# Means sent for a step sooner, a query pair turned by VectorE, wo rounded behind the gated tiles

## The chip, the cores and the metric

The kernel runs on one core of a Trainium2 chip. A core has five engines with a queue each: TensorE (PE, with its weight loads shown apart as PEld), VectorE (DVE), ScalarE (ACT), GpSimd (POOL) and SyncE (SP, which issues DMAs only). The metric is the device time of one execution in microseconds (us), lower is better.

## The reference

Two blocks read the same layer-normed input, and both are added to it. S = 2048 rows, D = 512, 32 heads of 16, the gated block 1376 wide.

```python
xn = _layernorm(x)
q, k, v = split(xn @ wqkv)                        # 32 heads of 16
phi(t)  = concat(softmax(t @ w_phi), softmax(-(t @ w_phi)))   # 32 features a head
kv  = einsum("bhsf,bhsd->bhfd", phi(k), v);  z = sum_s phi(k)
o   = (phi(q) @ kv) / (phi(q) . z + 1e-6)
A   = o @ wo
u   = gelu(xn @ w_in);  z1, z2 = halves of u;  z2 = _layernorm(z2)
B   = (z1 * (w_sp @ z2 + b_sp)) @ w_out           # w_sp mixes the 2048 rows
out = x + A + B
```

## The kernel before

Rows go in 16 tiles of 128 (NT = 16), two of them form a pair. Every product of the reference is made in three matmuls (helper `mm3`, lines 56 to 58): high by high, high by low, low by high, where the high half is ScalarE's rounding (`round_h`, L48) and the low half VectorE's rest (`rest_l`, L52). So each tile that PE reads has two halves.

**Phase 1** (the loop over s with `proj_k`, `proj_q`, `proj_v`, `z1_raw`) makes the features of keys and queries and sums up kv and z. From some tile on, x comes transposed from DRAM (`lay_x`), and the mean is taken off it by an accumulating DMA: `send_mean(s)` computes the negative mean (the tiles named mask in the traces) and SP stores it to `nm_d`; `center_t(s)` issues on POOL's queue a DMA that adds `nm_d` to the laid tile (xc<-nm_d, L318); then ACT and DVE split it into xT. The query features without their denominator go to DRAM by `proj_q` (e_d<-e on POOL, L336), and `add_kv` adds the key features into zacc by a DMA on POOL (L342).

**The middle** multiplies w_in for z, normalises it and splits it into B tiles. There the first NE = 2 tiles of query features are loaded back, divided by their denominator (`q_fin`), and stored to e_d again (L647). Then the loop over n (NC steps) multiplies w_sp by z2, in the form of seven products P1 to P7 in PSUM banks (`products`, the tiles g), which `drain` combines into c (L771 to L776). `gate` multiplies by z1, and its `turn` transposes the result on VectorE (L795) and stores it in blocks of 32 by 32 to u_d (L798), on POOL's queue for one pair and on SP's for the others. Near the loop's end `first_gate`, `first_q` (eq<-e_d, L835) and `stage_w` load what the last phase starts with.

**The last phase** makes out, tile by tile: `project_u` multiplies the gated tile by w_out (pout<-wu, the first of them with u_uh and ul_rt), `attend_T` turns a pair's features on PE (ptq, L934 and L936) and copies them on ACT to f (L938), `attend` multiplies f by kv (po, L951) and splits the result into the two halves of oT (ACT L48 and DVE L52), and `project_o` adds oT by wo to the same PSUM bank (pout<-woh,oT) and sends it out (xr, L983, and out<-xr on POOL). `features` runs `q_fin` for the tiles ahead on DVE (L542 to L549), and for most of them POOL copies the result to a tile of its own (er<-et, L905). wo's rows are loaded and split (wof, woh, wol) behind a point that `issue_after` names.

Two things set the order of the work. Within an engine the program's order of rows is fixed at build time by a scheduler, which `issue_after` holds back. And the on-chip memory is given out by pools: the last phase's pool `wk` (named cwk, two buffers a tag unless said otherwise) gives its addresses in the order in which tags are first requested, over memory that earlier pools held. Before the last phase that memory held, among others, `z1t` of the pool gt. A tile that lies over an older one waits for everything that still reads it. The empty requests (`wk.tile(...)` without use) are there to set that order.

Of the kernel before, what the change touches and what calls it, by code (L numbers as in the profile page):

```python
# [10 lines left out]
F32 = mybir.dt.float32  # L11
F32R = mybir.dt.float32r
# [6 lines left out]
P = 128  # L19
# [21 lines left out]
def mixer(ctx: ExitStack, tc: tile.TileContext, x, x_t, wv, wqkT, phi_bd, wo, w_in, wst, b_r, w_out, out):  # L41
# [36 lines left out]
    u_d = dram.tile([NT, FU, P], F32, name="u_d")  # L78
    kvT_d = dram.tile([P, D], F32, name="kvT_d")
    zb_d = dram.tile([P, NF], F32, name="zb_d")  # L80
    nm_d = dram.tile([NT, ND, P], F32, name="nm_d")

    ident = cst.tile([P, P], F32, name="ident")
# [13 lines left out]
    def heads(ap):  # L97
        return ap.rearrange("p (h d) -> p h d", d=DH)
# [76 lines left out]
    with ExitStack() as p0:  # L175
# [138 lines left out]

        def center_t(s):

            with tc.issue_after(send_mean.last):
                pool.dma_start(lay[s], nm_d[s].rearrange("c t -> (c t)").unsqueeze(0).to_broadcast([P, D]), accum_op=ALU.add)  # L318

        def keep_v(s, p):  # L320
# [12 lines left out]

        def proj_q(s):
            e = softmax_pair(wk, proj(s, wqk_h[:, 0], wqk_l[:, 0]), "q", r_x[:, s:s + 1])
            pool.dma_start(e_d[s], e)  # L336

        def add_kv(s, er):

# [142 lines left out]
        keep(pe=zproj.last)  # L482
        spare.update(zip((2, 3, 4, 5, 8, 9), [bd_t] + wkT_t + wqT_t[:1] + [None] * 2))
        n1, nq = 1, 0
        for s in range(NT):
            if s + 4 < FT:
                fetch(s + 4)
            if FT <= s + 6 < NT:
                fetch(s + 6)
            if FT <= s + 4 < NT:  # L490
                lay_x(s + 4)
            er = ek[s] if s < len(ek) else proj_k(s)
            if 1 < s < FT - 2:
                centered(s + 2)
            elif FT - 2 <= s < NT - 2:
                with tc.issue_after(softmax_pair.last[0]), tc.issue_after(softmax_pair.last[1]):
                    split_x(lay.pop(s + 2))
            if FT <= s + 4 < NT:
                send_mean(s + 4)
            if FT <= s + 3 < NT:  # L500
                center_t(s + 3)
            while nq < (s - 2) * NT // (NT - 3):
                proj_q(nq)
                nq += 1
            add_kv(s, er)
            if s == 0:
                tiles = fold_tiles(((za, "z"), (ps, "mm")))
                keep(pe=fold(0, wqT, tiles))
                folded(0, tiles)
            elif s == 1:  # L510
                proj_v(3)
            elif 2 < s < NT - 1:
                proj_v(s + 1)
            while n1 < s * (NT - LAG) // (NT - 1):
                z1_raw(wk, za, n1, 2)
                n1 += 1
            if s == 3:
                queue.close()
# [19 lines left out]
    def q_fin(et, tmp, zb):  # L538

        e, r, t, w = et[:, :NF], *(et[:, NF + k * 2 * H:NF + (k + 1) * 2 * H] for k in range(3))  # L540
        den = et[:, NF + 6 * H:QW]
        dve.tensor_tensor(tmp, e, zb, op=ALU.mult)  # L542
        dve.tensor_reduce(t, heads(tmp), axis=AX.X, op=ALU.add)
        dve.tensor_tensor(t, t, r, op=ALU.mult)
        dve.scalar_tensor_tensor(den, pairs(t, 0), EPS_DEN, pairs(t, 1), op0=ALU.add, op1=ALU.add)
        dve.reciprocal(den, den)
        dve.tensor_tensor(w.rearrange("p (h a) -> p h a", a=2), r.rearrange("p (h a) -> p h a", a=2),
                          den.unsqueeze(2).to_broadcast([P, H, 2]), op=ALU.mult)
        return e, dve.tensor_tensor(heads(e), heads(e), bc(w, 2 * H), op=ALU.mult).ins  # L549

    QC = 4
    NQ = NT // QC
# [45 lines left out]
    with ExitStack() as p1:  # L598
        tmp1 = p1.enter_context(left("tmp1", 1))
        kvT = tmp1.tile([P, D], F32, name="kvT")  # L600
        zb = tmp1.tile([P, NF], F32, name="zb")
        zhl = tmp1.tile([P, 4, D], F32R, tag="zhl", name="zhl")
        psk = p1.enter_context(psum("psk", 2))

        def make_zb():

            ones_r = tmp1.tile([P, P], F32R, name="ones_r")
            round_h(act, ones_r, ones)
            for k in range(2):
                pz = psk.tile([P, D], F32, tag="kvt", name="pz")  # L610
                cs = slice(k * D, (k + 1) * D)
                h, l = (zhl[:, 2 * k + n] for n in range(2))
                round_h(act, h, zacc[:, cs])
                rest_l(l, zacc[:, cs], h)
                pe.matmul(pz, ones_r, h, start=True, stop=False)
                pe.matmul(pz, ones_r, l, start=False, stop=True)
                dve.tensor_copy(zb[:, cs], pz)

        def make_kvT():
            kvm = zw.tile([P, 4, FC], F32, tag="T", name="kvm").rearrange("p a b -> p (a b)")[:, :D]  # L620
            kvm = kvm.rearrange("p (g b) -> p g b", b=P)
            dve.tensor_tensor(kvm.rearrange("p g (k b) -> p g k b", k=2),
                              kv_acc.unsqueeze(2).to_broadcast([P, NG, 2, HP]),
                              mask.rearrange("p (k b) -> p k b", k=2).unsqueeze(1).to_broadcast([P, NG, 2, HP]),
                              op=ALU.mult)
            pt = psk.tile([P, NG, P], F32, tag="kvt", name="kvt")
            for g in range(NG):
                pe.transpose(pt[:, g], kvm[:, g], ident)
            act.activation(kvT, pt.rearrange("p g b -> p (g b)"), AF.Copy)

        for j in range(2):
            load_win(w2[j], 2 + j)
        for s in range(NT - LAG, NT):
            z1_raw(tmp1, (za, zbp)[s % 2], s, 2)
            if s == NT - LAG + 1:
                make_zb()
        make_kvT()
        raw[0], raw[1] = load_a(0), load_a(1)
        A[0] = prep_a(0, raw.pop(0))
        sp.dma_start(kvT_d, kvT)  # L640
        sp.dma_start(zb_d, zb)
        tb = p1.enter_context(left("tmp1b", 1))
        for s in range(NE):
            et = load_q(s, tb.tile([P, QW], F32, name="et") if s else tmp1.tile([P, 4, D], F32, tag="zhl", name="et").rearrange("p a b -> p (a b)")[:, :QW])
            tmp = zw.tile([P, 4, FC], F32, tag="z2", bufs=2, name="qtmp").rearrange("p a b -> p (a b)")[:, :NF]
            e, _ = q_fin(et, tmp, zb)
            early = sp.dma_start(e_d[s, :, :NF], e).ins  # L647
    ctx_w1.__exit__(None, None, None)
    ctx_zc = psum("zc", 1)
    zc = ctx_zc.__enter__()  # L650
# [179 lines left out]

    lasts, wu = [None] * 9, []

    def first_q(s):
        e = slot("eq", F32R)[:, :NF]
        sp.dma_start(e.bitcast(F32), e_d[s, :, :NF])  # L835
        return e

    def stage_w():
        t = [xz2.tile([P, SL], F32, tag="b", name="wof") for _ in range(3)]
        w = [xz_tile(2 * D, F32R, "wu") for _ in range(KF + 1)]  # L840
# [8 lines left out]
    for n in range(NC):  # L849
        i = SEQ[n][0]  # L850
        if n % NQ == 1 and i < NP - 1:
            z = load_z1(i)
        products(n, g)
        if n % NQ == NQ - 1 and i < NP - 1:
            c = gt.tile([P, 2, FU], F32, tag="c", name="c")
            cq = c[:, :, :FH].rearrange("p k (j f) -> p k j f", j=2)
            cb = drain(i, g, cq)
            g = {}
        if n + 3 < NC:
            raw[n + 3] = load_a(n + 3)  # L860
        if n + 2 < NC:
            A[n + 2] = prep_a(n + 2, raw.pop(n + 2))
        if n % NQ == NQ - 1 and i < NP - 1:
            turn = gate(i, cb, z, c, z, prep_a.last)
            if i < NP - 2:
                turn()
        if n == NC - 4:
            stage_w()
        if n == NC - 3:
            zs = slot("zb", F32R)  # L870
            zb, ident_r = zs[:, :NF].bitcast(F32), zs[:, NF:NF + P]
            round_h(act, ident_r, ident)
            sp.dma_start(zb, zb_d)
            uT = [first_gate(0)]
            ets[2] = load_q(2, slot("et"))
            es[2], last = q_fin(ets.pop(2), slot("qtmp")[:, :NF], zb)
        if n == NC - 2:
            es[0], es[1] = first_q(0), first_q(1)
            t = xz_tile((KF + 1) * P, F32R, "u1")
            us = {1: load_u(1, k_tiles(t[:, :KF * P]).bitcast(F32), t[:2 * REM, KF * P:(KF + 1) * P])}  # L880
    cb = drain(NP - 1, g, slot("c").rearrange("p (k j f) -> p k j f", k=2, j=2))
# [108 lines left out]

    GATE_LAST = 8

    fT = attend_T(0)
    wk.tile([P, D], F32, tag="xr", bufs=3, name="xr")
    wk.tile([P, 10 * QP], F32, tag="gap", name="gap")
    wk.tile([P, NG, 2 * P], F32R, tag="oTh", name="oT")
    with tc.issue_after(lasts[5]), tc.issue_after(lasts[1]), tc.issue_after(fin[-1]):
        for c in range(ND):
            rows = [(m * QP, (m + 1) * QP) for m in range(c // 2 * 8 + c % 2, (c // 2 + 1) * 8, 2)]
            load_w(wo, rows, wo_h[:, c], wo_l[:, c], cw.tile([P, D], F32, tag="wof", bufs=4, name="wof"))  # L1000
# [77 lines left out]
```

## Time and profile before

| | before |
|---|---|
| median of 3 runs | 626.11 us |
| lowest and highest | 625.36 and 626.4 us |
| the profiled execution, its own time | 625.34 us |
| its span in the profile | 623.6 us |
| mean granted clock of TensorE | 0.999 |
| DVE, ACT, POOL busy | 508.3, 272.8, 113.7 us |

The span is the time from the first to the last instruction; the execution takes 1.7 us more around it. A row of the timeline gives start, length, engine, line, operation and tiles, with the idle time before it and what ended it in brackets. A row of the chain of waits gives start, length and what it was. In a row by windows come the stretch, its length, busy time and count for PE, PEld, DVE, ACT and POOL, the granted clock, the busy share of the DMA engines and GB/s. In a group's row stand count, busy time and mean of one in ns, or least, median and largest ns; "DMA to landing" goes from issue to the last byte. Matmuls overlap: their starts, not their lengths, tell the pace.

### The profile page before, as it was taken

The numbers are of one execution on the slowest core, as the hardware profiler recorded it, in microseconds if no ns is written. First come the engines' busy times: TensorE is split into PE (matmuls) and PEld (weight loads), VectorE is DVE, ScalarE is ACT, GpSimd is POOL, SyncE is SP. The second block draws the span as 40 slices with busy tenths as digits, with TensorE's granted clock in tenths as the row PEclk, the third lists the DMA queues.
The fourth block names the chain that finished last, engine by engine and source line by source line (L and its number), as shares of the span: only waits on it lengthen the run. The fifth ranks groups of instructions, "written<-read, shape, count | busy, mean of one in ns | idle before, by whom it ended". The sixth has DMA issues, their size and how long they took to land.

```text
span 623.6 us, 11439 instructions
## 1 busy us (share of the span) xinstructions
PE 615.1 (99%) x4366; PEld 561.5 (90%) x4366; DVE 508.3 (82%) x903; ACT 272.8 (44%) x436; POOL 113.7 (18%) x198
## 2 busy tenths in 40 slices
PE   8999999999999999999999999999999999999997
PEld 7888888878889999999999999999999887788785
DVE  5999899899988498988989888696959899989211
ACT  4652324333433558876435433253444433334331
POOL 4122233222211025541000000000000212211110
PEclk9999999999999999999999999999999999999999
DMA  9557676566546757002464745637477799984722
GB/s 318 189 138 165 162 183 187 152 165 172 118 154 186 271 210 270 2 1 67 129 128 136 196 89 155 156 97 173 88 177 244 225 284 332 328 243 111 162 38 48
DMA packets 90671, 103.67 MB, mean 166 GB/s; under 512 B 47080, under 2 KB 60136, under 8 KB 90376
## 3 DMA queue, kind: packets, MB, share of 16 engines
q1 hardware_dynamic: 76840, 60.76, 34.0%
q0 software_dynamic: 11472, 36.54, 23.6%
q10 hardware_dynamic: 2304, 5.64, 2.4%
q8 instruction: 34, 0.56, 0.4%
q14 instruction: 21, 0.17, 0.1%
HBM read 61.61 MB, written 30.56 MB: 148 GB/s over the span
## 4 chain that ended last, share of the span: by engine, by line
PE 85%; DMA 6%; DVE 4%; issue 3%; POOL 1%; ACT 1%; DVEq 0%; POOLq 0%
PE g L58 11%; PE g L57 10%; PE g L56 10%; PE zps L58 6%; PE zps L56 6%; PE zps L57 6%; PE pout L56 5%; PE pout L58 5%; PE pout L57 5%; DMA xc<-nm_d 5%; PE proj L56 4%; PE proj L57 4%; PE proj L58 4%; PE ptq L936 1%; PE po L951 1%
## 5 line engine op out<-in xcount | busy, mean ns | idle before, releaser
L57 PE MATMUL g<-B,A 128*128 128x344 f32 x448 | 143.4, 320 | 0.0
L56 PE MATMUL g<-B,A 128*128 128x344 f32 x448 | 142.9, 320 | 0.0
L58 PE MATMUL g<-B,A 128*128 128x344 f32 x448 | 140.7, 321 | 0.1
L56 PEld LDWEIGHTS g<-B,A 128*128 128x128 f32 x448 | 84.3, 188 | 0.0
L57 PEld LDWEIGHTS g<-B,A 128*128 128x128 f32 x448 | 84.2, 188 | 0.0
L58 PEld LDWEIGHTS g<-B,A 128*128 128x128 f32 x448 | 83.7, 188 | 0.4 <-DVE A L52 0.4
L48 ACT ACTIVATE A<-S 128x512 fp32r<-128x512 f32 x64 | 39.2, 629 | 76.3 <-DVE S L588 61.3
L121 ACT ACTIVATE e<-e,r_x 128x1024 f32<-128x1024 f32 x26 | 29.9, 1150 | 56.3 <-DVE e L120 55.1
L56 PE MATMUL proj<-wqk_h,xT 128*128 128x512 f32 x128 | 50.1, 391 | 0.0
L57 PE MATMUL proj<-wqk_l,xT 128*128 128x512 f32 x128 | 50.0, 390 | 0.0
L58 PE MATMUL proj<-wqk_h,xT 128*128 128x512 f32 x128 | 49.9, 390 | 0.0
L48 ACT ACTIVATE A<-wf 128x512 fp32r<-128x512 f32 (+1 forms) x64 | 33.1, 519 | 33.3 <-DMA wf<-in_wst 12.6
L52 DVE TENSOR_TENSOR A<-S,A 128x512 fp32r<-128x512 f32 x64 | 43.0, 686 | 4.4 <-ACT A L48 4.0
L56 PE MATMUL zps<-w_0h,xT 128*128 128x344 f32 x128 | 41.1, 321 | 0.0
L56 PE MATMUL zps<-w_1h,xT 128*128 128x344 f32 x128 | 40.9, 319 | 0.0
L58 PE MATMUL zps<-w_0h,xT 128*128 128x344 f32 x128 | 40.8, 319 | 0.0
L58 PE MATMUL zps<-w_1h,xT 128*128 128x344 f32 x128 | 40.7, 319 | 0.0
L57 PE MATMUL zps<-w_1l,xT 128*128 128x344 f32 x128 | 40.6, 318 | 0.0
L57 PE MATMUL zps<-w_0l,xT 128*128 128x344 f32 x128 | 40.6, 318 | 0.0
L753 POOL DMA_DIRECT2D z1t<-z_d x16 | 8.6, 545 | 166.9 <-DMA u_d<-z1t 124.9
L52 DVE TENSOR_TENSOR A<-wf,A 128x512 fp32r<-128x512 f32 (+1 forms) x64 | 35.0, 549 | 1.8 <-ACT A L48 1.8
L124 DVE TENSOR_REDUCE sm<-e 128x64 f32<-128x1024 f32 x26 | 31.2, 1200 | 1.7 <-ACT e L121 1.5
(218 smaller groups left out, 1430.6 us busy)
## 6 DMA issues: line engine op xcount, KB each, us to landing
wf<-in_wst SPq DMA_DIRECT2D x64, 256.0 KB, 3.1
e_d<-e POOLq DMA_DIRECT2D x16, 544.0 KB, 5.0
et<-e_d SPq DMA_DIRECT2D x16, 544.0 KB, 5.2
er<-et POOLq DMA_DIRECT2D x12, 512.0 KB, 5.5
z_d<-z1f ACTq DMA_DIRECT2D x16, 344.0 KB, 2.3
z1t<-z_d POOLq DMA_DIRECT2D x16, 344.0 KB, 5.3
zacc<-e POOLq DMA_DIRECT2D x10, 512.0 KB, 4.7
u<-u_d SPq DMA_DIRECT2D x15, 320.0 KB, 6.3
```

The lines of the kernel that those rows point to most:

```text
L48: return act.activation(h, src, AF.Copy).ins
L52: return (eng or dve).tensor_tensor(l, src, h.bitcast(F32), op=ALU.subtract).ins
L56: pe.matmul(dst, ah, bh, start=start, stop=False)
L57: pe.matmul(dst, ah, bl, start=False, stop=False)
L58: return pe.matmul(dst, al, bh, start=False, stop=stop).ins
L121: softmax_pair.last = less, act.activation(e, e, AF.Exp, scale=scale).ins
L124: dve.tensor_reduce(sm, heads(e), axis=AX.X, op=ALU.add)
L753: pool.dma_start(t[:, k, :FH], z1_d[2 * i + k])
L936: pe.transpose(pt[:, a, k].bitcast(F32R), src, ident_r)
L951: lasts[3] = pe.matmul(po[r][c * QP:(c + 1) * QP, k], kvT[rows, m // 2, cols], fs[m // 4][rows, m // 2 % 2], start=True, stop=True).ins
```

## The change

```diff
+    q_d = dram.tile([NP, NF, 2, P], F32, name="q_d")
...
         def center_t(s):
-            with tc.issue_after(send_mean.last):
+            with tc.issue_after(send_mean.last), tc.issue_after(proj_q.last or send_mean.last):
                 pool.dma_start(lay[s], nm_d[s].rearrange("c t -> (c t)").unsqueeze(0).to_broadcast([P, D]), accum_op=ALU.add)
...
-            pool.dma_start(e_d[s], e)
+            proj_q.last = pool.dma_start(e_d[s], e).ins
...
+        proj_q.last = None
         for s in range(NT):
...
-            if FT <= s + 3 < NT:
-                center_t(s + 3)
             while nq < (s - 2) * NT // (NT - 3):
                 proj_q(nq)
                 nq += 1
+            if FT <= s + 4 < NT:
+                center_t(s + 4)
...
+    def turn_q(s, dst, e, eng=sp):
+        ins = dve.transpose(dst, e).ins
+        q = q_d[s // 2, :, s % 2].rearrange("(m j) t -> j m t", j=BL)
+        for b in range(0, P, BL):
+            turn_q.last = eng.dma_start(q[:, :, b:b + BL], dst[b:b + BL].rearrange("p (m t) -> p m t", t=BL)).ins
+        return ins
+
+    def load_f(s, f, g):
+        sp.dma_start(f, q_d[s // 2, 2 * g * P:2 * (g + 1) * P].rearrange("(a p) k t -> p a (k t)", p=P))
+        return f
...
-            e, _ = q_fin(et, tmp, zb)
-            early = sp.dma_start(e_d[s, :, :NF], e).ins
+            done.append(q_fin(et, tmp, zb)[0])
+        for s in range(NE):
+            turn_q(s, done[s - 1] if s else zb, done[s])
+        early = turn_q.last
...
-    def first_q(s):
-        e = slot("eq", F32R)[:, :NF]
-        sp.dma_start(e.bitcast(F32), e_d[s, :, :NF])
-        return e
...
-            es[0], es[1] = first_q(0), first_q(1)
+            fT = []
+            for k in range(0, NG, 2):
+                t = slot("f")[:, :NF].rearrange("p (g a t) -> p g a t", g=2, a=2)
+                fT += [load_f(0, t[:, j], k + j) for j in range(2)]
...
-    fT = attend_T(0)
     wk.tile([P, D], F32, tag="xr", bufs=3, name="xr")
     wk.tile([P, 10 * QP], F32, tag="gap", name="gap")
     wk.tile([P, NG, 2 * P], F32R, tag="oTh", name="oT")
-    with tc.issue_after(lasts[5]), tc.issue_after(lasts[1]), tc.issue_after(fin[-1]):
+    with tc.issue_after(lasts[0]), tc.issue_after(lasts[1]), tc.issue_after(fin[-1]):
```

It has three parts. **The means:** `center_t` is called for tile s + 4, in the same step as its `send_mean`, behind `proj_q` instead of ahead of it, and for one tile ahead of what it was. **The first pair's query features:** the two tiles that `q_fin` divides early are turned on VectorE in blocks of 32 by 32 (into zb and into the first tile's own place) and stored by four DMAs each to `q_d`, 32 by 32 block by block, so that `q_d` holds them turned. At the loop's end four loads bring them as f, where two loads brought the features unturned, and `attend_T(0)` is gone: 16 transposes of PE and 4 copies of ACT. **wo:** the issue point of its rows names the rounding of the last gated tile (`lasts[0]`) and no longer the copy of f (`lasts[5]`, gone).

With `attend_T(0)` gone, the five buffers of the tag f (2,048 bytes each, in every partition) are first requested behind xr, gap and oT instead of ahead of them. In bytes from the start of a partition, the pieces around it are:

| tile | before | after |
|---|---|---|
| z1t of pool gt (older) | 195,040 to 200,928 | the same |
| high half of oT, first pair | 201,120 to 205,216 | 190,880 to 194,976 |
| low half of oT, first pair | 209,312 to 213,408 | 199,072 to 203,168 |
| xr, first | 192,416 to 194,464 | 182,176 to 184,224 |

The first place of the order is phase 1 on POOL: one step with its zacc, e_d and the mean (mask), and the DMA that adds the mean. Before:

```order
L342 DMA zacc<-wrow 128x1024
L336 DMA e_d<-e 128x1088
L311 TENSOR_SCALAR mask<-mask 128x32
L94 TENSOR_SCALAR mask<-mask 128x1
L318 DMA xc<-nm_d 128x512
L95 TENSOR_TENSOR r_x<-mask,mhalf 128x1
L342 DMA zacc<-e 128x1024
```

And in the changed kernel:

```order
L312 TENSOR_SCALAR mask<-mask 128x32
L95 TENSOR_SCALAR mask<-mask 128x1
L96 TENSOR_TENSOR r_x<-mask,mhalf 128x1
L319 DMA xc<-nm_d 128x512
L343 DMA zacc<-e 128x1024
```

The xc row stood between a mask and r_x and adds the mean of the tile before; it now stands behind r_x and adds the mean that the mask rows right above it made.

The second place is PE at the end of the loop over n: the last product (g), the turning of the first pair (ptq) and the first tile of out (pout). In brackets stand the semaphores that a row waits for. Before:

```order
L58 MATMUL g<-B,A 128x344
L936 MATMUL ptq<-zb,eq 128x128 [waits DMAHW6_49,DVE_49]
L936 MATMUL ptq<-zb,eq 128x128 [waits DMAHW7_49]
L936 MATMUL ptq<-zb,eq 128x128 x2
L936 MATMUL ptq<-zb,eq 128x128 [waits DVE_49]
L936 MATMUL ptq<-zb,eq 128x128 x7
L936 MATMUL ptq<-zb,eq 128x128 [waits Activation_49]
L936 MATMUL ptq<-zb,eq 128x128 x3
L56 MATMUL pout<-wu,u_uh 128x512
L57 MATMUL pout<-wu,u_uh 128x512
```

And in the changed kernel:

```order
L56 MATMUL g<-B,A 128x344
L57 MATMUL g<-B,A 128x344
L58 MATMUL g<-B,A 128x344
L56 MATMUL pout<-wu,u_uh 128x512 [waits DVE_49,Activation_49]
L57 MATMUL pout<-wu,u_uh 128x512
L58 MATMUL pout<-wu,ul_rt 128x512
```

The transposes are gone, and the first pout follows the last product; it waits for DVE and ACT, which free its PSUM bank and write its operands.

The third place is DVE where it writes the low half of oT for the first pair, between the split of wo (wol) and the features of tile 3 (qtmp<-et). A wait named DMASW is one for a DMA of POOL's queue. Before:

```order
L52 TENSOR_TENSOR wol<-wof,woh 128x512 [waits DMAHW2_49,DMAHW1_49,DMAHW7_49,DMAHW0_49,Activation_49]
L52 TENSOR_TENSOR oT<-po,oT 128x2x256 [waits Activation_49] x2
L542 TENSOR_TENSOR qtmp<-et,zb 128x1024 [waits DMAHW3_49]
L52 TENSOR_TENSOR ul<-u,uh 128x640 [waits DMAHW4_49,Activation_49]
L543 TENSOR_REDUCE et<-qtmp 128x64 [waits DVE_49]
```

And in the changed kernel:

```order
L52 TENSOR_TENSOR wol<-wof,woh 128x512 [waits DMAHW2_49,DMAHW1_49,DMAHW7_49,DMAHW0_49,Activation_49]
L52 TENSOR_TENSOR oT<-po,oT 128x2x256 [waits DMASW1_49,DMASW2_49,DMASW0_49,DMASW3_49,DVE_49,Activation_49]
L52 TENSOR_TENSOR oT<-po,oT 128x2x256 [waits Activation_49]
L544 TENSOR_TENSOR qtmp<-et,zb 128x1024 [waits DMAHW3_49]
L52 TENSOR_TENSOR ul<-u,uh 128x640 [waits DMAHW4_49,Activation_49]
L545 TENSOR_REDUCE et<-qtmp 128x64 [waits DVE_49]
```

The rows stand in the same order. The first write of oT has gained waits for four DMAs of POOL's queue, which are the four stores u_d<-z1t of `turn` (L798 before, L814 now).

More of the change, by code (lines that the diff above doesn't have):

```diff
@@ L641, in mixer @@
         sp.dma_start(zb_d, zb)
-        tb = p1.enter_context(left("tmp1b", 1))
+        tb, done = p1.enter_context(left("tmp1b", 1)), []
         for s in range(NE):
```

## The prediction

> **What bounds the kernel now.** The page's first part comes first, then the waits of PE.
>
> ```profile
> PE 615.1 (99%) x4366; PEld 561.5 (90%) x4366; DVE 508.3 (82%) x903; ACT 272.8 (44%) x436; POOL 113.7 (18%) x198
> ```
> ```profile
> PE proj L56 <- ACT xT L48: 1.2, 1, 1.2
> PE ptq L936 <- DVE c L771: 0.8, 1, 0.8
> ```
>
> PE is busy 99% of the span, and after the first matmul its named waits are 1.2 and 0.8 us. So a gain can come only from these two, from a shorter idle that no row names, or from PE work removed. A loss can come from any new wait of PE, since nothing on PE hides one. The time is therefore read on PE's timeline (start, length, instruction; in brackets the idle before and what ended it). The profiled execution took 625.34 us, its span is 623.6; the median of the runs is 626.11, so what I sum against 625.34 gets 0.8 added at the end.
>
> **Part 1: the mean is accumulated a step sooner.** PE's timeline, a piece of the chain of waits, and POOL's timeline, around the second wait:
>
> ```profile
> 126.07 0.39 PE L58 MATMUL proj<-wqk_h,xT 128*128 128x512 f32 x1
> 127.68 0.50 PE L56 MATMUL proj<-wv_h,xT 128*128 128x512 f32 x1 [1.22 <-ACT xT L48]
> 128.02 0.39 PE L57 MATMUL proj<-wv_l,xT 128*128 128x512 f32 x1
> 128.25 0.32 PE L56 MATMUL zps<-w_0h,xT 128*128 128x344 f32 x1
> ```
> ```profile
> 121.44 5.53 DMA xc<-nm_d
> ```
> ```profile
> 106.46 0.32 POOL L311 TENSOR_SCALAR mask<-mask 128x32 f32<-128x32 f32 x1 [1.01 <-DVE mask L310]
> 107.03 0.92 POOL L318 DMA_DIRECT2D xc<-nm_d  x1
> ...
> 118.57 0.87 POOL L342 DMA_DIRECT2D zacc<-er  x1 [8.20 <-ACT v L322]
> ...
> 120.87 0.32 POOL L311 TENSOR_SCALAR mask<-mask 128x32 f32<-128x32 f32 x1
> ```
>
> The accumulation issued at 121.44 is for the tile whose mean was ready at 106.46; it stands behind the mask of the following tile (120.87). Matmuls of this shape start 0.23 us apart (128.02 to 128.25), so 127.68 - 126.07 - 0.23 = 1.4 us are lost, and the first restart is 0.34 instead of 0.23: 1.5 us. After the change the accumulation goes out behind the mask of its own tile and the store of it, some 10 us earlier, and PE's next proj finds xT ready: **-1.5 us**. The bounds are -1.5 (all of it) and 0 (the wait is only exchanged for another in this stage, where DVE is nearly as full as PE). POOL now waits for the store of the mean (its landing is not shown apart; between 0 and the 5.5 us of the accumulation itself), and behind that wait on POOL stand zacc and e_d. The rows above put the next zacc 11.5 us after the accumulation (118.57 against 107.03), so the wait is over before POOL is wanted: nothing.
>
> **Part 2: VectorE turns the first pair's features.** In the stage of z, two 128x1024 transposes are added on DVE, and eight stores of 128-byte pieces replace two of whole rows.
>
> ```profile
> L795 DVE STREAM_TRANSPOSE z1t<-c 128x1472 f32<-128x1472 f32 x7 | 11.9, 1704 | 0.0
> ```
> ```profile
> 230.00:290.00 60.00, 60.00 (x383) 60.00 (x382) 52.86 (x107) 48.04 (x74) 25.65 (x45) 1.00 0.27 92
> ```
> ```profile
> 229.12 3.66 SPq L647 DMA_DIRECT2D e_d<-et  x2
> ```
> ```profile
> 242.47 0.77 ACT L48 ACTIVATE B<-T 128x688 fp32r<-128x688 f32 x1
> ```
> ```profile
> L798 SPq DMA_DIRECT2D u_d<-z1t x4: 330/1148/1544, 318.1 to 320.8; - x4
> ```
>
> A transpose of 1472 columns takes 1.70 us, so 1024 take an estimated 1.2, twice: 2.4 us. DVE (fourth group of the row by windows: 52.86 of 60) has 7 us free there, and PE none, so this is hidden: 0, with +2.4 as the bad end if DVE were late just then. The stores read the tiles that ACT overwrites from 242.47 on. Four stores of the same 128-byte kind and 184 KB each were issued in 2.7 us; the new ones are 128 KB each, begin about 231 and should have landed before 242. Cost 0; bad end about +2.
>
> At the end of the kernel, 16 transposes of PE and four copies of ACT go.
>
> ```profile
> 490.17 0.46 PE L936 MATMUL ptq<-zb,eq 128*128 128x128 f32 x4
> 491.39 1.23 PE L936 MATMUL ptq<-zb,eq 128*128 128x128 f32 x12 [0.77 <-DVE c L771]
> 492.46 0.46 PE L56 MATMUL pout<-wu,u_uh 128*128 128x512 f32 x1
> ```
> ```profile
> 489.73 0.52 DVE L776 TENSOR_TENSOR c<-g,c 128x344 f32<-128x344 f32 x1
> ```
>
> The first pout starts at 492.46, after four transposes, the wait and twelve more. Without them it needs a PSUM bank that DVE's L776 frees at 490.25, so it starts about 490.35: **-2.1 us**. The wait for L771 (0.8) is not replaced.
>
> ```profile
> 478.07 3.61 SPq L835 DMA_DIRECT2D eq<-e_d  x2
> ```
>
> The f tiles now come from DRAM in four loads of half the size, issued where the two eq loads stood and used at 494.4, 12 us behind; hidden.
>
> **Part 3, and what comes with part 2: a new wait.** wo's loads are no longer held by ACT's copies; ACT and DVE round them where they did, so this edit alone costs and brings 0. But the order in which the last pool's tiles are first requested changes. The five f buffers (10,240 bytes) used to come ahead of xr and oT, and now come behind. The low half of oT moves from bytes 209,312 on to 199,072 on, and there it overlaps the last z1t (195,040 to 200,928). Four stores u_d<-z1t still read that tile, so DVE's first row that writes oT now waits for all four (`DMASW0` to `DMASW3` in DVE's rows in the section on the change). When do they land?
>
> ```profile
> 494.06 3.63 POOL L798 DMA_DIRECT2D u_d<-z1t  x4 [36.90 <-ACT woh L48]
> ```
> ```profile
> L798 POOL DMA_DIRECT2D u_d<-z1t x2: 900/904/907, 495.9 to 496.8; - x2
> ...
> DMA to landing us min/median/max: 8.2/8.6/9.0
> ```
> ```profile
> 498.34 1.29 DVE L52 TENSOR_TENSOR oT<-po,oT 128x512 fp32r<-128x512 f32 x2 [1.32 <-ACT oT L48]
> 499.54 1.22 DVE L542 TENSOR_TENSOR qtmp<-et,zb 128x1024 f32<-128x1024 f32 x1
> ...
> 505.48 1.22 DVE L542 TENSOR_TENSOR qtmp<-et,zb 128x1024 f32<-128x1024 f32 x1
> ```
> ```profile
> 502.48 0.39 PE L58 MATMUL pout<-woh,oT 128*128 128x512 f32 x1
> ```
>
> The last two stores are issued at 495.9 and 496.8 and need 8.2 to 9.0 us, so the last lands between 505.0 and 505.8. I take 505.1, the short end, since the two landings of a queue that drains evenly lie close. Their start follows from DVE's transpose behind the drain of g, which the change does not move against g's end. DVE then writes the first low half (0.65), ready at about 505.9, and PE can go on at 506.0. PE needs it at the fifth matmul with wo (L58 at 502.48), now 2.1 earlier, 500.4. **+5.6 us** on PE. If the stores landed at the first one's pace (5.5 us: 502.3), it would be +2.8; at 505.8, +6.3.
>
> DVE stands too: its next work, features(3) (L542), starts at 505.1 + 0.1 + 1.2 = 506.4 instead of 499.54, 6.9 later. PE, by then 5.6 - 2.1 = 3.5 later than before, meets that delay again at the first transposes of pair 4:
>
> ```profile
> 514.45 1.23 DVE L549 TENSOR_TENSOR et<-et 128x1024 f32<-128x1024 f32 x1
> ```
> ```profile
> 516.25 0.54 POOL L905 DMA_DIRECT2D er<-et  x1 [4.76 <-issue]
> ```
> ```profile
> L905 POOL DMA_DIRECT2D er<-et x1: 537/537/537, 516.2 to 516.2; - x1
> ...
> DMA to landing us min/median/max: 6.5/6.5/6.5
> ```
> ```profile
> 523.28 1.47 PE L936 MATMUL ptq<-zb,er 128*128 128x128 f32 x16
> ```
>
> Before, features(5) ended at 515.68, its copy er was issued at 516.25 and landed 6.5 later, 522.75, and PE wanted it at 523.28: slack 0.5. After, three features take 515.68 - 499.54 = 16.1 us from 506.4, and the two writes of the next pair's low half (1.3) now stand ahead of the end of features(5): 523.8, issue 524.4, landing 530.9. PE wants it at 523.28 + 3.5 = 526.8, and has four of the 16 transposes (0.37) to do without it: 530.9 - 527.1 = **+3.8 us**. With the median of all such copies (5.5) it is 2.8, with their extremes (3.2 and 9.4) 0.5 and 6.7. Pair 2's own twelve transposes want features(3) at 513.7 and get it at 512.4. After pair 4 PE is about 7 us later than before and DVE about 8, so nothing further is late.
>
> **A smaller idle.** One matmul at 297.85 starts 0.3 late behind DVE:
>
> ```profile
> 297.41 0.32 PE L57 MATMUL g<-B,A 128*128 128x344 f32 x1
> 297.85 0.43 PE L58 MATMUL g<-B,A 128*128 128x344 f32 x1
> ```
>
> DVE's order there changes (one add of the drain goes behind an A<-S); I take **-0.3**, between 0 and -0.4.
>
> **Sum.** 625.34 - 1.5 - 2.1 - 0.3 + 5.6 + 3.8 = 630.8; with 0.8 for the median, 631.6 us.
>
> **A rule weighed: the clock.** The kernel's start shows what PE does after rest: the first two matmuls start 0.73 and 0.51 apart, where 0.23 is the pace later.
>
> ```profile
> 6.72 0.80 PE L56 MATMUL proj<-wv_h,xT 128*128 128x512 f32 x1
> 7.45 0.67 PE L57 MATMUL proj<-wv_l,xT 128*128 128x512 f32 x1
> 7.96 0.40 PE L58 MATMUL proj<-wv_h,xT 128*128 128x512 f32 x1
> ```
>
> No idle after that is longer than 1.5 us, so no row shows whether a stall of 5.6 us brings the slow pace back. If 3.4 us of matmuls ran at half pace after it, PE would be 1.7 later; behind the first stall that only eats into the second, behind the second it adds 1.7: 633.3. The Trainium skill (TensorE: Matmul & The Clock Gate, Part 1) states such a rule: an idle window of about 3.4 us halves the clock, and a busy one of the same length restores it. By it the sum would be near 633.3, without it 631.6.
>
> **The rivals.**
> - The gains alone: the stores land before PE wants the low half, that is before about 499.6. For it: part 1 and part 2 are on PE's own path, 3.9 us. Against it: even the first store, issued at 494.06, needed 5.5, and DMA moved the last ones in over 8. Time 625.34 - 3.9 + 0.8 = **622.2**. Chance 0.17. This is the case on the other side; it decides at a landing before 499.6, and it breaks even (626.1) when the stores land at about 503.4 and the copy of pair 4 costs nothing.
> - The first stall alone: DVE makes up its delay, or the copy of er lands in 3.2 us. 622.2 + 5.6 = **627.8**, and 629.5 at half pace. Chance 0.17.
> - The half pace behind both stalls: **633.3**. Chance 0.13.
> - Part 1 doesn't do what it says: POOL, waiting for the store of the mean, delays zacc and e_d, and with them the softmax of phase 1; its 1.5 comes back and the 2 of the bad ends are added: **633 to 636**. Chance 0.08.
> - The forecast, both stalls: **631.6**. Chance 0.45.
>
> The range reaches from the gains alone, 621.8, to 636. A measurement of this kernel can tell about 0.2% from no change, 1.25 us. Faster by more: the gains alone and a little of landings in between, 0.19. Within: 0.07. Slower: 0.74.
>
> **What would show it.** Part 1: no bracket at PE's first proj<-wv near 126, POOL's xc<-nm_d ahead of the next mask. Part 2: the first pout about 2.1 us nearer to the last g, with no ptq between. The new wait: PE's first woh L58 with some 5 us of idle ended by DVE oT L52, and DVE idle before it ended by the DMA u_d<-z1t; then a bracket of 1 to 4 us at the first transposes of pair 4. I am wrong if DVE's first write of oT waits for ACT alone, or if the stores land before 500.

## The result, and the profile after

| | before | changed |
|---|---|---|
| median of 6 runs each | 625.74 us | 631.36 us |
| lowest and highest | 624.79 to 626.47 | 629.86 to 632.05 |
| ratio, 95% interval | | 1.0085 [1.0066, 1.0104] |
| profiled execution, span | 625.34, 623.6 | 630.46, 628.8 |
| mean granted clock of PE | 0.999 | 0.994 |

Slower by 0.85%, as forecast: 631.36 where 631.6 was predicted. That the two agree to 0.2 us is luck: three of the terms behind the number were off, and their errors nearly cancel. The experiments below are mostly about these. First the waits of PE in the changed kernel (engine, tile, line, what it waited for: us in total, times, longest):

```profile
PE pout L58 <- DVE oT L52: 5.7, 1, 5.7
PE idle L383 <- POOL ident masks.py:199: 1.8, 1, 1.8
PE g L56 <- ACT A L48: 0.9, 1, 0.9
PE zps L56 <- ACT z1f L152: 0.5, 1, 0.5
```

Both waits of before, at proj and at ptq, are gone, and three new ones stand there; the 1.8 at the start (idle) is there before the change, too. PE's timeline of the changed kernel shows each place:

```profile
126.01 0.39 PE L58 MATMUL proj<-wqk_h,xT 128*128 128x512 f32 x1
126.24 0.39 PE L56 MATMUL proj<-wv_h,xT 128*128 128x512 f32 x1
...
220.50 0.43 PE L56 MATMUL zps<-w_0h,xT 128*128 128x344 f32 x1 [0.48 <-ACT z1f L152]
...
489.88 0.32 PE L58 MATMUL g<-B,A 128*128 128x344 f32 x1
490.04 0.40 PE L56 MATMUL pout<-wu,u_uh 128*128 128x512 f32 x1
...
499.76 0.39 PE L57 MATMUL pout<-wol,oT 128*128 128x512 f32 x1
505.86 0.80 PE L58 MATMUL pout<-woh,oT 128*128 128x512 f32 x1 [5.72 <-DVE oT L52]
506.45 0.63 PE L56 MATMUL pout<-woh,oT 128*128 128x512 f32 x1
506.88 0.63 PE L57 MATMUL pout<-wol,oT 128*128 128x512 f32 x1
...
508.96 0.39 PE L56 MATMUL pout<-woh,oT 128*128 128x512 f32 x1
...
528.28 1.47 PE L950 MATMUL ptq<-zb,er 128*128 128x128 f32 x16
```

No idle is left near 126. The first pout follows the last g in 0.16 us, where before it took 492.46 - 490.01 = 2.45. Then PE stands 5.7 us, and behind that the matmuls start 0.43 apart instead of 0.23 until about 509. The transposes of pair 4 (528.28) run without a wait. What PE waits for is on DVE's timeline, and in the row of the four stores:

```profile
505.12 1.29 DVE L52 TENSOR_TENSOR oT<-po,oT 128x512 fp32r<-128x512 f32 x2 [8.61 <-DMA u_d<-z1t]
506.32 1.22 DVE L544 TENSOR_TENSOR qtmp<-et,zb 128x1024 f32<-128x1024 f32 x1
```
```profile
L814 POOL DMA_DIRECT2D u_d<-z1t x4: 900/910/947, 493.5 to 496.2; - x4
...
DMA to landing us min/median/max: 6.4/7.2/8.8
```

DVE stood 8.61 us, until the store issued at 496.2 had landed 8.8 later. The slow matmuls have the granted clock beside them, in the view by windows (the third column from the end):

```profile
500.00:502.00 2.00, 0.14 (x1) 0.00 (x0) 0.00 (x0) 0.43 (x1) 0.00 (x0) 1.00 0.99 303
502.00:504.00 2.00, 0.00 (x0) 0.00 (x0) 0.00 (x0) 0.30 (x1) 0.00 (x0) 0.52 1.04 310
504.00:506.00 2.00, 0.14 (x1) 0.14 (x1) 0.89 (x2) 0.00 (x0) 0.00 (x0) 0.50 1.15 286
506.00:508.00 2.00, 2.00 (x5) 1.61 (x6) 2.00 (x3) 0.00 (x0) 0.00 (x0) 0.50 0.64 209
508.00:510.00 2.00, 2.00 (x8) 1.59 (x8) 2.00 (x3) 0.00 (x0) 0.00 (x0) 0.78 0.20 61
```

The column is the mean of a stretch, so the moment of a fall can be worked out: 0.52 from 502 to 504 is 1.92 of the 2 us at half. The clock fell at about 502.1 and, by the 0.78 from 508 to 510, came back at about 508.9.

### The profile page after: what moved, and what is told of

Its sections match the earlier page's. It is cut to its first block, busy times and chain, and to the rows that moved or that the text cites. A ratio compares the mean times of both kernels' runs of the same rounds, so it can differ in the third digit from the quotient of the medians.

```text
span 628.8 us, 11407 instructions
## 1 busy us (share of the span) xinstructions
PE 615.1 (98%) x4350; PEld 560.7 (89%) x4350; DVE 509.3 (81%) x905; ACT 269.0 (43%) x432; POOL 114.4 (18%) x198
## 4 chain that ended last, share of the span: by engine, by line
PE 81%; DMA 5%; POOL 4%; issue 4%; DVE 3%; ACT 2%; SPq 1%; POOLq 0%; DVEq 0%; ACTq 0%
PE g L58 10%; PE g L56 10%; PE g L57 10%; PE proj L56 7%; PE proj L57 7%; PE proj L58 7%; PE pout L56 5%; PE pout L58 5%; PE pout L57 5%; PE zps L56 3%; PE zps L58 3%; PE zps L57 3%; POOL rstd L96 2%; DMA wf<-in_wst 1%; DMA u_d<-z1t 1%
```

## The experiments

All runs of a group share their runs of before, 23 to 29 of them; ratios are to these, and more executions show a wider spread of before (622.63 to 629.75 in the first group) than the first six did.

**keep_layout: the overlap taken out.** The changed kernel with

```diff
+    for _ in range(NG):
+        wk.tile([P, 2, 2 * P], F32, tag="f", bufs=NG + 1, name="f")
     wk.tile([P, D], F32, tag="xr", bufs=3, name="xr")
```

> The changed kernel, with the f buffers asked for ahead of xr, gap and oT as before, so that the low half of oT lies where it lay and no longer over z1t. The rows of every engine stay in the order of the changed kernel. Theory (the overlap is what costs): the stall of 5.7 us at PE's first L58 of wo and the slow pace behind it (about 1.5) go, 631.4 - 7.2 = 624.2. Rival A (PE meets the next late thing, the copy of er of pair 4, which had 0.5 us of slack before): a stall of 1 to 2 us there, about 625.5. Rival B (the low half of oT is late for another reason): stays above 630.

625.98 us, 0.9998 [0.9977, 1.0018]. The stall is gone, and 5.4 us with it; for the rest rival A has the place right, at pair 4. PE's timeline shows the wait, and POOL's and DVE's what came ahead of it:

```profile
523.75 0.46 PE L950 MATMUL ptq<-zb,er 128*128 128x128 f32 x4
525.13 1.22 PE L950 MATMUL ptq<-zb,er 128*128 128x128 f32 x12 [0.93 <-DMA er<-et]
```
```profile
521.46 0.56 POOL L919 DMA_DIRECT2D er<-et  x1 [5.70 <-issue]
```
```profile
501.07 1.23 DVE L544 TENSOR_TENSOR qtmp<-et,zb 128x1024 f32<-128x1024 f32 x1 [0.75 <-DMA et<-e_d]
...
506.74 0.83 DVE L52 TENSOR_TENSOR ul<-u,uh 128x640 fp32r<-128x640 f32 x1 [1.99 <-ACT uh L48]
```

The copy itself was quick here, 3.6 us from issue to landing where it took 6.5 before. It was issued late, because features(5) ended only at 520.9: DVE had waited 0.75 for a load of et and, with a third wait of 0.50, 2.5 for ACT, which itself waited for loads of u. Before, DVE has none of these waits between 499.54 and 515.68. So what runs out of slack is a chain of loads, features and copy, of which the copy is the last link.

**layout_only: the overlap alone.** The kernel before, with the order of the requests changed and nothing else:

```diff
-    fT = attend_T(0)
     wk.tile([P, D], F32, tag="xr", bufs=3, name="xr")
     wk.tile([P, 10 * QP], F32, tag="gap", name="gap")
     wk.tile([P, NG, 2 * P], F32R, tag="oTh", name="oT")
+    for _ in range(2):
+        wk.tile([P, NG, 2 * P], F32R, tag="oTl", name="oT")
+    fT = attend_T(0)
```

> The kernel before with nothing changed but the order in which the last pool's tags are first asked for: the f buffers behind xr, gap and both halves of oT, so that the low half of oT lies over z1t as in the changed kernel. All engines' rows stay in the order of before. Theory (the overlap is the cause of the loss): DVE's first low half waits for the stores, to about 505; PE, here 2.1 later at its fifth matmul with wo than in the changed kernel, stands about 3.5 us, and the clock falls about 2 us into the rest and stays low 6.8 us, which costs 2 to 2.5 more: 631 to 632. Rival (a rest of 3.5 is too short for the clock): 629.5. Other rival (the loss comes from another part of the change): 626.

632.71 us, 1.0109 [1.009, 1.0128]: the whole loss of the change, and more, from where a tile lies. The timelines of PE and DVE, and the view by windows:

```profile
502.69 0.39 PE L57 MATMUL pout<-wol,oT 128*128 128x512 f32 x1
507.83 0.79 PE L58 MATMUL pout<-woh,oT 128*128 128x512 f32 x1 [4.76 <-DVE oT L52]
508.43 0.63 PE L56 MATMUL pout<-woh,oT 128*128 128x512 f32 x1
```
```profile
507.09 1.29 DVE L52 TENSOR_TENSOR oT<-po,oT 128x512 fp32r<-128x512 f32 x2 [9.90 <-DMA u_d<-z1t]
```
```profile
504.00:506.00 2.00, 0.00 (x0) 0.00 (x0) 0.00 (x0) 0.00 (x0) 0.00 (x0) 1.00 1.08 328
506.00:508.00 2.00, 0.17 (x1) 0.17 (x2) 0.91 (x2) 0.00 (x0) 0.00 (x0) 0.50 1.10 298
508.00:510.00 2.00, 2.00 (x5) 1.61 (x6) 2.00 (x3) 0.00 (x0) 0.00 (x0) 0.50 0.33 114
...
512.00:514.00 2.00, 2.00 (x9) 1.59 (x8) 1.97 (x4) 0.60 (x1) 0.60 (x1) 0.79 0.41 123
```

DVE waits for the same four stores. The stall was 4.8 us where 3.5 was expected (the stores landed up to 9.7 us behind their issue here), and the low clock lay later than in the changed kernel, so that 5 us of matmuls ran in it (507.8 to 512.8) and not 3: 2.5 us lost by that alone.

**fill_stall: PE kept busy in the stall.** The changed kernel with

```diff
+        if not i:
+            t = pst.tile([P, D], F32, tag="tr", name="idle")
+            with tc.issue_after(lasts[2]):
+                for _ in range(25):
+                    j = pe.matmul(t, uT[1][0][:, 0], wu[0][0], start=True, stop=True, skip_group_check=True).ins
         for k in range(2):
-            project_o(i + k, oT, p.pop(i + k))
+            with tc.issue_after(lasts[2] if i else j):
+                project_o(i + k, oT, p.pop(i + k))
```

> The changed kernel, with 25 more matmuls of 128x512 on PE (their result is not read) between the second pout by w_out and the first by wo, about 5.7 us, that is in the place of the stall. Theory (the slow pace behind the stall comes from PE's rest): the granted clock stays at 1.00, the matmuls behind start 0.23 apart, and the time falls by 1.5 to 629.9. Rival (the slow pace comes from operands or DMA traffic just then): the pace and the time stay, 631.4.

638.53 us, 1.0196 [1.0163, 1.023]. As a time it is a miss: the scheduler, which reckons the 25 matmuls in, put later rows of DVE in another order, and two new waits came (0.6 and 3.1), with a fall of the clock behind the longer one. As a test of the clock it serves, by PE's timeline and the clock at both places:

```profile
504.84 0.39 PE L57 MATMUL pout<-wol,oT 128*128 128x512 f32 x1
507.15 0.50 PE L58 MATMUL pout<-woh,oT 128*128 128x512 f32 x1 [1.92 <-DVE oT L52]
507.49 0.40 PE L56 MATMUL pout<-woh,oT 128*128 128x512 f32 x1
507.73 0.39 PE L57 MATMUL pout<-wol,oT 128*128 128x512 f32 x1
...
524.57 0.39 PE L57 MATMUL pout<-wol,oT 128*128 128x512 f32 x1
528.03 0.79 PE L58 MATMUL pout<-woh,oT 128*128 128x512 f32 x1 [3.08 <-DVE oT L52]
528.62 0.63 PE L56 MATMUL pout<-woh,oT 128*128 128x512 f32 x1
529.05 0.63 PE L57 MATMUL pout<-wol,oT 128*128 128x512 f32 x1
```
```profile
506.00:508.00 2.00, 0.85 (x4) 0.71 (x5) 1.60 (x3) 0.00 (x0) 0.00 (x0) 1.00 1.05 268
...
526.00:528.00 2.00, 0.00 (x0) 0.00 (x0) 1.90 (x7) 0.00 (x0) 0.00 (x0) 0.80 0.43 156
528.00:530.00 2.00, 1.97 (x5) 1.58 (x6) 2.00 (x2) 0.00 (x0) 0.34 (x1) 0.50 1.04 363
...
532.00:534.00 2.00, 2.00 (x6) 1.58 (x5) 1.86 (x6) 0.00 (x0) 0.00 (x0) 0.50 0.85 184
534.00:536.00 2.00, 2.00 (x13) 1.62 (x12) 2.00 (x2) 0.71 (x2) 0.85 (x2) 0.99 1.01 339
```

Matmuls of one shape, by the same wo, for two pairs: at full pace where PE had rested 1.9 us, at half where it had rested 3.1. The rival with the DMA traffic fails: the DMA engines' share was 1.05 at the place with the full pace. The slow pace comes from the rest.

**means_only and means_again: part 1 alone,** the lines of `center_t`, `proj_q` and the loop over s put into the kernel before.

> The kernel before with the part on the means alone. Theory: the idle of 1.2 us near 126 goes, but PE then waits near 220 for ACT, which stands behind a load of wf that does not come sooner (0.5 to 0.6 back), net -0.9: 624.8. Rival: the 1.5 stays whole to the end, 624.2. Other rival: all of it comes back at later loads of the middle, 625.7.

> The part on the means alone once more, beside the other two on one chip: 624.0, 0.35% under before, and the smallest spread of executions. Rival (the first comparison was luck): 0.1% or less under before.

624.01 us, 0.9965 [0.9947, 0.9982], and 624.12 us, 0.9971 [0.9957, 0.9986]. Part 1 is worth 2.2 and 1.8 us by the ratios, 2.3 and 1.45 by the medians. The intervals together reach from 0.9 to 3.3, so that it is worth more than the 1.5 that one trace of before shows is not shown. In the first profile 0.9 comes back near 220, in the second nothing does, so that wait differs by execution.

**turn_keep: parts 2 and 3 without overlap and means,** keep_layout with `center_t(s + 3)` where it was.

> The changed kernel without the part on the means and with the f buffers asked for first, so parts 2 and 3 alone without the overlap. Theory: PE starts the first pout 2.1 us sooner; 623.6 if nothing takes it back, 624.6 if the idle of 0.9 near 292 (g behind ACT A L48, behind a load of wf) belongs to this part. Rival: that idle belongs to PE being early from the means, then it is not here.

627.9 us, 1.0032 [1.001, 1.0054]: slower. Parts 2 and 3, forecast at -2.1, cost 2.0 us by the ratio and 1.6 by the medians. The profiled execution was its fastest (624.82) and shows the wait near 292 (1.0), so that one can come without part 1; but its twelve executions fall in two groups, six from 624.8 to 627.3 with a mean clock of 0.998 or more, and six from 628.5 to 630.1 with 0.995 or 0.996. One fall of 6.8 us, as in the changed kernel, takes 3.4 of some 625 us, 0.0054, off the mean clock; a mean of 0.998 comes without any, from the end of the span, where PE has no work (before_nc5's trace: 0.82 and 0.50 in the windows from 620 to 624). So 0.996 or less is read here as one fall, after a long rest somewhere; no trace shows such an execution of these kernels, so this is worked out and not seen. The next four runs look for where.

**no_turn and er_act: the two suspects.** Each changes one line of keep_layout:

```diff
-        ins = dve.transpose(dst, e).ins
+        dst = e
```
```diff
-        lasts[6] = pool.dma_start(es[s].bitcast(F32), e).ins
+        lasts[6] = (act if s in (4, 5) else pool).dma_start(es[s].bitcast(F32), e).ins
```

> keep_layout without the two transposes of DVE in the stage of z (the eight stores stay, and write the features unturned, so the first pair's part of the output is left out in this sense). Theory (their 2.4 us on DVE make DVE free the buffer of wf later, and with it the load that PE waits for near 292): the wait of g for ACT A near 292 is gone or under 0.3, and the time 0.8 to 1.0 below keep_layout, 625.1. Rival (the eight stores in SP's queue, or the new order of rows, make it late): the wait stays at 0.8 to 1.0 and the time at 626.

> keep_layout with the copies er<-et of tiles 4 and 5 issued on ACT's queue instead of POOL's. Theory (pair 4's transposes wait for the copy of tile 5, which has no slack left once PE is 2 us earlier, and in some executions stand long enough for the clock to fall): the wait at ptq<-zb,er near 525 goes, the long executions of 628 to 630 with a mean clock of 0.994 to 0.996 go, and the median is 1 below keep_layout, 625. Rival (the features on DVE end too late, whichever queue copies them): the wait stays at about 1 and the time at 626.

no_turn: 625.68 us, 0.9992 [0.9973, 1.0012]. The wait near 292 is gone from its trace. Over all traces, that wait is in none of the seven of kernels without the transposes on DVE, and in six of the seven of kernels with them, at 0.3 to 1.1 us (turn_nc5, below, has none); so the transposes do bring it, but not in every execution. Half of no_turn's executions still have a clock of 0.994 to 0.996, and the median hardly moves. er_act: 625.28 us, 0.9983 [0.997, 0.9995]. No execution with a clock under 0.998 is left, though 0.8 of the wait is. So the long rests seem to be those for the copy of er, though the longest wait for it in any trace is 1.3 (no_turn); and on ACT's queue, too, the copy comes late (6.3 us to landing in its trace).

**no_copy5 and no_copy5_no_turn: no copy to wait for.**

```diff
-        if s == 3:
+        if s in (3, 5):
             return
```

> keep_layout with tile 5's features left in the place where DVE makes them, as tile 3's are, so that pair 4's transposes wait for DVE and no longer for the copy er<-et of tile 5 (8 of the 16 transposes then go by the unrounded identity). Theory (that copy is the next late thing once the overlap is gone, by 0.8 to 1.3 in the profiles and by enough for the clock to fall in the long executions): no wait of PE near 520 to 525, no execution with a mean clock under 0.998, median 1 to 1.5 below keep_layout's 626.0, 624.7. Rival (part 2's loss lies in the middle, near 292 and in the drains): 625.7 or more.

> no_copy5 without the two transposes on DVE in the stage of z (the first pair's features are stored unturned). Theory (these two causes together are part 2's whole loss): PE waits neither near 292 nor near 520, and the time is that of the means alone less the 2.1 of the sixteen transposes, 624.0 - 2.1 = 621.9, at most 622.9. Rival (a third cause): 623.5 or more.

no_copy5: 622.45 us, 0.9953 [0.9936, 0.997], eleven of twelve executions between 621.8 and 623.3. It is 3.1 us below before, where the changed kernel is 5.6 above, below means_again in the same group (624.12), and 2.2 below the 624.7 that was expected. The twelfth execution (627.07) has a clock of 0.995, where none under 0.998 was expected, so a long rest can still come without this copy. Its waits of PE, but for the 1.8 at the start:

```profile
PE g L56 <- ACT A L48: 0.9, 1, 0.9
PE g L56 <- DVE c L792: 0.3, 1, 0.3
```

The one at er is gone, the one near 292 is still there. Without the transposes (no_copy5_no_turn, 622.49 us, 0.9952 [0.9933, 0.9971]) that one goes too, and the median stays: what is won near 292 is not seen at the end. The median lies within the expected bound of 622.9 and 0.6 above the 621.9 itself; why is left open. In sum, keep_layout, turn_keep and no_turn, with the copy on POOL's queue, have 15 of 36 executions with a clock of 0.996 or less; er_act, these two runs and turn_nc5 below, with the copy on ACT's queue or gone, have 2 of 44. One reservation: with tile 5's copy gone, the scheduler also reorders DVE's rows of the tiles behind it, so these runs don't part the copy from that order; er_act, which keeps the copy on another queue, has none of the long executions either, but a median (625.28) far above theirs.

**before_nc5 and turn_nc5: how much of that belongs to the change.** The same line in the kernel before and in turn_keep.

> The kernel before with tile 5's features left where DVE makes them, as in no_copy5. Theory (before the change the copy had 0.5 us of slack, as its profile shows, so it is no late thing there): the same time, within 0.2% of before. Rival (in many executions of before the copy is late as well, and its wide spread comes from that): 1 to 2 us less and a narrower spread, and then no_copy5 owes that much not to the change.

> turn_keep (parts 2 and 3 without the overlap and without the means) with tile 5's features left where DVE makes them. Theory (part 2 is worth its 2.1 us less 0.9 near 292 once the copy is out of the way): 1.2 to 2 below before, and no execution with a mean clock under 0.998. Rival (part 2 loses elsewhere): as before or slower.

before_nc5: 625.66 us, 0.9981 [0.9963, 0.9999]; three executions of before with a clock of 0.995 to 0.997 (628.3 to 630.6) have no counterpart in it. That the copy is late now and then in the kernel before too may be so, but it isn't shown: in all four groups only 3 of 100 executions of before have a clock of 0.996 or less, so that twelve without one say little. turn_nc5: 624.5 us, 0.9976 [0.9957, 0.9995], none with a clock under 0.998. It is below before_nc5 by 1.2 us in the medians, but by 0.0005 only in ratios whose intervals overlap: with the copy out of the way parts 2 and 3 lose nothing any more; how much they gain is not settled by this pair.

| medians, us | parts 2 and 3 without overlap | and part 1 |
|---|---|---|
| with the copy of tile 5 | 627.9 (before 626.31) | 625.98 |
| without it | 624.5 (before_nc5 625.66) | 622.45 (its before 625.57) |

## Why the prediction was right, and where it was not

- **The overlap and the stall: right in mechanism, place and size.** Predicted: DVE held until 505.1, PE's fifth matmul with wo at 506.0, +5.6 on PE. Measured: 505.12, 505.86, 5.7 idle. That the points in time agree as well is luck: the prediction read them off the timeline of before without its own -1.5 and -0.3, and in the trace the waits near 220 and 292 took these back, so that the last g starts at 489.88 against 490.01. The size of the stall doesn't hang on that. layout_only shows that the overlap alone does it, keep_layout that without it the loss is gone.
- **The slow clock: mis-sized, because put in the wrong place.** The prediction had it as a rival with 0.13, and argued that behind the first stall it would only eat into the second. It came behind the first, and cost (508.96 - 505.86) - 7 x 0.23 = 1.5 us, near the 1.7 given; the second stall was not there for it to eat into. The slow rows at the start of the kernel (6.72 to 7.96), on which the prediction leaned, don't show such a fall: the view by windows has a granted clock of 1.00 there, and PE had been at work since 1.82.
- **The second stall, at pair 4: wrong, +3.8 for 0.** DVE's part of that step held: features(5) ended at 523.5 (523.8 predicted) and the copy was issued at 524.04 (524.4). The step that failed is the 6.5 us from issue to landing, taken from the same copy before. It was 3.0 in the changed kernel:

```profile
L919 POOL DMA_DIRECT2D er<-et x1: 556/556/556, 524.0 to 524.0; - x1
...
DMA to landing us min/median/max: 3.0/3.0/3.0
```

  It landed at 527.04, and PE came at 528.28, 1.5 later than the 526.8 of the sum, which is the slow clock. With a landing of 6.5 (530.5) PE, which has four transposes to do without the copy, would have stood 1.9: about half of the 3.8 went with the landing, the rest with PE's later and the copy's earlier start. One transfer of the profile was taken for its rule, though the prediction itself names the extremes of such copies, 3.2 and 9.4. In other traces the same copy took 3.6 (keep_layout), 5.2 (turn_keep), 5.6 (no_turn) and 6.3 (er_act). The time goes with how busy the DMA engines were while it ran: their share was 0.66 in the changed kernel and 0.84 in keep_layout, but 1.08 in turn_keep, 1.07 in no_turn, 1.06 in er_act and 1.03 before. Why they were less busy in two of them is open: a stall of PE is not needed, since keep_layout has none.
- **Part 1: right.** The idle near 126 went, -1.5 in the trace. What the prediction didn't have is that PE, being early, waits 0.5 near 220 for ACT, whose row stands behind a load of wf that does not come sooner; about half of the gain is given back there in this execution. POOL waited 3.9 us for the store of the mean, which the prediction allowed for, and its next zacc waited for DVE, so nothing was lost there.
- **Part 2: right at its place, wrong in its sum.** The first pout came 2.3 sooner against the last g (2.1 predicted). Two of the things that the prediction held to be covered were not. The transposes of 2.4 us on DVE were "hidden" by 7 us of free time in the stage, but free time of a stage is not free time at its end. The chain of waits of the changed kernel there:

```profile
289.04 0.43 DVE S L605
289.47 0.02 issue
289.49 3.19 DMA wf<-in_wst
292.68 0.02 issue
292.70 0.64 ACT A L48
```

  S frees the buffer of wf at 289.47 (the same row ended at 287.01 before), a load of 3.2 us follows, and PE waits 0.9 for ACT behind it; no_turn, without the transposes, has no such wait. The stated bad end, +2.4, covers it; the value taken, 0, did not. And the slack of 0.5 us at pair 4, which the prediction read and used for the stalled case, is smaller than the 2.1 that PE gains: in the rival of the gains alone (622.2) the gain would not have arrived. keep_layout is that case, and gave 626.0, there with features(5) late as well.
- **The 0.3 near 297** went, as predicted, in the trace of the changed kernel.

In the profiled executions: 625.34, - 1.5 near 126, - 0.3 near 297, + 0.7 near 220 and + 1.1 near 292 (idle and slow restart), - 2.3 at the first pout, + 5.9 stall, + 1.5 clock = 630.4, and 630.46 was measured. The forecast had 630.8 from - 3.9, + 5.6 and + 3.8. So the total was right with the second stall too high by 3.8, and the clock and the two waits in the middle left out by 3.3.

## What to carry to other kernels

- An edit that removes a step also removes its requests for memory. Where a pool gives addresses in the order of first requests, compare the addresses and the waits of the next tiles; here that cost more than all the edit's gains together, and empty requests in the old place mend it.
- Before a gain on the critical engine is counted, read the slack of what it will meet next. At 99% busy, 2 us gained met a chain of loads, features and a copy with 0.5 us to spare, and the version that also takes the copy away is the one that pays (0.9953).
- A landing time read once is one value of a spread (3.0 to 6.5 us here for one copy); a term that hangs on it needs both ends.

## What the runs showed of the hardware

The granted clock of PE fell to a half in three traces, in rests of 5.7 us, of 4.8 and of 3.1, and not in one of 1.9. From the end of the last matmul to the fall it took 1.9 us (500.15 to 502.1), 2.9 (503.1 to 506.0) and 2.2 (525.0 to 527.2), and it stayed low for 6.8 us each time (502.1 to 508.9, 506.0 to 512.8, 527.2 to 534.0), whether PE worked in most of that time or in less than half. The Trainium skill (TensorE: Matmul & The Clock Gate, Part 1) has a free-running window of 3.4 us, after which an idle PE goes to half rate and a busy one back. The spread of 1.9 to 2.9 fits a window that runs free, and 6.8 is two of its windows; but the fall came after less than a whole window of rest, and a rest of 3.1 us was enough. By these traces, then, the limit lies between 1.9 and 3.1 us. A stall beyond it cost itself and half of what was left of the 6.8 us when the matmuls came back: 1.5 us in the changed kernel, 2.5 in layout_only and 3.0 in fill_stall. Three traces are few, and the mean clocks of the other executions of the changed kernel and layout_only (0.993 to 0.997) suggest that the low stretch was not as long in each.
